# Window attention on one core: a new order of the stages in a slot, and smaller loads

## The chip, the cores and the metric

The kernel runs on one core of one Trainium2 chip. The metric is the device time of that core in microseconds (us). Before the change it is 4291.93 us, the median of 3 runs (4291.89 to 4298.81). All times below are of runs in the fast state, except one single run, whose state is unknown and which is marked. Most results are given as a ratio with a 95% interval, against runs of the kernel before on the same chip in the same rounds.

## The reference

```
x : (1, 511, 511, 192) bf16       window 7 x 7, 4 heads of 48
xp = pad(x, 1 on each side)
x0 = x + sum over i, j of xp[i : i+H, j : j+W] * dw_pe[i, j]      # depthwise 3x3
h  = layernorm(x0)                                                  # over the 192 channels
q, k, v = windows_of(h) @ w_qkv                                     # 73 x 73 windows of 49 tokens
out = softmax(q k^T / sqrt(48)) v,  @ w_o,  back to the image
return x0 + out
```

## The kernel before

Up to 128 windows lie on the 128 partitions and make a **block**. There are 42 blocks: 41 full or nearly full ones, and a ragged one of 81 windows. A block is worked off in 16 **slots** of 8 windows (11 in the last), 667 slots in all. While slot by slot the attention of block b runs, the same slots carry the convolution and then the LayerNorm (LN) of block b+1, and SyncE issues the loads of block b+2. The stages of a slot have letters in the code: A0 and A1 make q and k, V the values, B the scores and their exponential, D the product of the probabilities with v (one slot late), E the transposition of its result o (two slots late).

```python
for g in range(NG + LE + 1):                  # one turn is one slot
    # ... f0, f: how far the slot is within its block, from 0 to 1
    pj = []
    if 1 <= b and ck >= LE:
        goal = 13 if b == NB else part(0.10, 0.68, 13)      # 13 projections of block b-1
        # ...
    def hook(share):        # statistics for VectorE, stores and loads for SyncE
        # ...
        if n and conv.c == C:
            n.stats(int(s_start + (s_goal - s_start) * share))
        # ...
            goal = part(0.45, 0.82, len(xp), at)              # patches, 18 loads
            # ...
                goal = part(0.80, 0.90, len(xl), at)          # x, 4 loads
    if g < NG:
        stage_A(b, ck, 0, fill)               # q; fill() puts convolution matmuls between
        hook(0.15)
    if 0 <= g - LE < NG:
        stage_E(*groups[g - LE], nc.vector.tensor_copy)
    if g < NG:
        stage_A(b, ck, 1, fill)               # k
        hook(0.35)
    for s0 in pj:
        proj(b - 1, s0, ...)
    hook(0.55)
    now[0] = g + 0.5
    if n and g < NG:
        n.transpose(part(0.57, 0.95, WS), 0.9)    # LN transpose T of one row of block b+1
    if 0 <= g - LD < NG:
        stage_D()
    if g < NG:
        stage_B()
        hook(0.75)
        stage_V(b, ck, fill, nc.scalar.copy)
        # ...
```

The loads. Each window lies on one partition of X. The image rows of the windows are loaded in two pieces per line of windows:

```python
def load_x(self, b):
    for r0, r1 in ((0, 4), (4, WS)):          # 4 rows of 7, then 3
        for p, at in self.strips(b, r0, r1):  # two lines of windows per block
            # ... one nc.sync.dma_start each: 672 KB or 504 KB
```

The LN of a row of windows takes statistics on VectorE, then three steps on GpSimd (`tensor_scalar`, `pow`, and the multiplication that gives h), then the transpose T on TensorE, whose result is copied into HO half by VectorE and half by ScalarE. The tensors of a slot share a ring of three double banks of PSUM (`PS`). T and the convolution have their own two banks.

## Time and profile before

| | before |
|---|---|
| time, median | 4291.93 us |
| TensorE busy, mean granted clock | 85%, 0.91 |
| time at half clock in the profiled run | 771 us of 4282.5 |
| blocks 1 to 34, mean | 97.1 us |
| blocks 35 to 38 (tall ones are loaded and worked on) | 109.5, 120.0, 115.8, 115.4 us |
| block 39 (the ragged one is loaded), block 40, the last to the end | 138.5, 99.0, 79.8 us |

Times of blocks and slots here and below come from the starts of the 667 exponentials in the trace: "interval 8" is the mean, over blocks 1 to 33, of the time from the exponential of slot 8 to that of slot 9; interval 15 leads into the next block. "Half clock" sums the stretches for which the trace records a granted clock below full speed.

Two more lines of the wait table of the kernel before matter later (engine, line and tile, what it waited for: us in total, times, longest):

```profile
PE ps L369 <- DVE o L438: 91.0, 207, 0.8
...
PE ps L407 <- ACT k L377: 29.4, 78, 0.7
```

They are small waits of 0.4 us each, five and two in a block: q waits for VectorE, which frees a PSUM bank with o, and the scores wait for the eviction of k. And these are the x loads on the page's list of DMA issues (tile and source, engine, times, KB each):

```profile
X<-in_x_dram SPq DMA_DIRECT2D x82, 672.0 KB
X<-in_x_dram SPq DMA_DIRECT2D x82, 504.0 KB
```

### The profile page before, as it was taken

The numbers are of one execution on the slowest core, as the hardware profiler recorded it, in microseconds if no ns is written. First come the engines' busy times: TensorE is split into PE (matmuls) and PEld (weight loads), VectorE is DVE, ScalarE is ACT, GpSimd is POOL, SyncE is SP. The second block draws the span as 40 slices with busy tenths as digits, with TensorE's granted clock in tenths as the row PEclk, the third lists the DMA queues.
The fourth block names the chain that finished last, engine by engine and source line by source line (L and its number), as shares of the span: only waits on it lengthen the run. The fifth ranks groups of instructions, "written<-read, shape, count | busy, mean of one in ns | idle before, by whom it ended". The sixth has DMA issues, their size and how long they took to land.

```text
span 4282.5 us, 166362 instructions
## 1 busy us (share of the span) xinstructions
PE 3637.9 (85%) x75049; PEld 3180.5 (74%) x75049; DVE 2548.2 (60%) x4238; ACT 2779.9 (65%) x3508; POOL 2061.2 (48%) x1428
## 2 busy tenths in 40 slices
PE   4888888888989898888888888888889987777867
PEld 3777777777777787777777777777777876666656
DVE  6665666665565666666566566666656655555534
ACT  1666676666666677767666666766766665555646
POOL 4244455554444455555444445555544444444434
PEclk9998999999898899999999899999988997888878
DMA  5233344444333334444333333444433333333211
GB/s 121 62 85 85 91 97 97 105 102 99 84 85 85 85 91 95 103 107 104 91 85 85 85 91 91 98 98 104 106 86 85 85 84 84 84 84 71 54 43 43
DMA packets 522734, 376.91 MB, mean 88 GB/s; under 512 B 447216, under 2 KB 447408, under 8 KB 522014
## 3 DMA queue, kind: packets, MB, share of 16 engines
q1 hardware_dynamic: 521548, 365.89, 37.3%
q8 instruction: 589, 9.65, 0.9%
q14 instruction: 131, 1.07, 0.1%
q10 hardware_dynamic: 466, 0.30, 0.0%
HBM read 265.31 MB, written 100.27 MB: 85 GB/s over the span
## 4 chain that ended last, share of the span: by engine, by line
PE 51%; POOL 15%; DVE 10%; ACT 9%; SPq 6%; issue 5%; DMA 3%; ACTq 0%; POOLq 0%; DVEq 0%
PE ps L369 17%; PE psc L314 10%; PE ps L385 8%; POOL h L337 6%; ACT pO L475 6%; PE ps L452 6%; SPq L236 5%; POOL X L479 4%; PE ps L464 4%; POOL rstd L335 4%; DVE o L438 3%; PE psc L347 3%; DMA X<-in_x_dram 3%; DVE bnst L325 2%; ACT k L377 2%
## 5 line engine op out<-in xcount | busy, mean ns | idle before, releaser
L479 POOL TENSOR_TENSOR X<-X,pO 128x768 bf16<-128x768 bf16 (+1 forms) x539 | 836.6, 1565 | 1855.5 <-ACT pO L475 1853.9
L369 PE MATMUL ps<-HO,Wqk 96*128 96x392 bf16 x5336 | 1454.5, 357 | 100.1 <-DVE o L438 91.0
L314 PEld LDWEIGHTS <-XP 81*128 81x128 bf16 x8064 | 1117.6, 176 | 254.0 <-issue 191.9
L314 PE MATMUL psc<-T,XP 81*128 81x49 bf16 x8064 | 1100.6, 220 | 141.4 <-DMA XP<-in_x_dram 53.9
L377 ACT CAST k<-ps 128x784 bf16<-128x784 f32 x667 | 541.8, 812 | 477.9 <-PE ps L369 456.1
L369 PEld LDWEIGHTS <-Wqk 96*128 96x128 bf16 x5336 | 605.3, 117 | 261.5 <-issue 159.6
L385 PE MATMUL ps<-Wv,HO 96*128 96x192 bf16 x5336 | 687.5, 259 | 122.9 <-ACT pO L475 95.4
L377 ACT CAST q<-ps 128x784 bf16<-128x784 f32 x667 | 544.0, 816 | 316.2 <-PE ps L369 266.5
L453 DVE COPY HO<-ps 96x784 bf16<-96x784 bf16 x667 | 381.9, 573 | 614.9 <-PE ps L452 551.2
L320 DVE TENSOR_TENSOR X<-psc,X 128x490 bf16<-128x490 f32 x840 | 541.4, 645 | 321.6 <-PE psc L314 257.6
L337 POOL TENSOR_TENSOR h<-X,rstd 128x1344 bf16<-128x1344 bf16 x291 | 707.7, 2432 | 22.8
L393 ACT CAST v<-ps 128x768 bf16<-128x768 f32 x667 | 536.7, 805 | 234.8 <-PE ps L385 211.8
L438 DVE TENSOR_TENSOR o<-ps,rs 128x768 bf16<-128x768 f32 x667 | 638.7, 958 | 23.5
L415 ACT ACTIVATE pt<-ps 128x784 bf16<-128x784 f32 x667 | 550.9, 826 | 124.1 <-PE ps L407 121.0
L385 PEld LDWEIGHTS <-HO 96*128 96x128 bf16 x5336 | 520.7, 107 | 122.5 <-issue 94.0
L357 DVE COPY HO<-psc 96x896 bf16<-96x896 bf16 x294 | 339.0, 1153 | 323.8 <-PE psc L347 322.1
L325 DVE BATCH_NORM_STATS2 bnst<-X 128x6 f32<-128x384 bf16 x1050 | 518.1, 547 | 3.0
L452 PEld LDWEIGHTS <-o 128*96 128x96 bf16 x5336 | 422.1, 137 | 53.8 <-issue 8.6
L452 PE MATMUL ps<-ident,o 128*96 128x128 bf16 x5336 | 456.2, 234 | 3.9 <-issue 2.5
L464 PE MATMUL ps<-Wo,HO 96*128 96x192 bf16 x4116 | 454.2, 260 | 0.8 <-DVE HO L453 0.7
L357 ACT COPY HO<-psc 96x896 bf16<-96x896 bf16 x294 | 324.1, 1102 | 194.1 <-PE psc L347 152.1
L335 POOL TENSOR_TENSOR rstd<-tmp,expo 128x7 f32<-128x7 f32 x294 | 436.7, 1485 | 24.5
(54 smaller groups left out, 2872.0 us busy)
## 6 DMA issues: line engine op xcount, KB each, us to landing
XP<-in_x_dram SPq DMA_DIRECT2D x568, 216.0 KB
out_dram<-X SPq DMA_DIRECT2D x246, 336.0 KB
X<-in_x_dram SPq DMA_DIRECT2D x82, 672.0 KB
X<-in_x_dram SPq DMA_DIRECT2D x82, 504.0 KB
XP<-in_x_dram SPq DMA_DIRECT2D x151, 212.6 KB
out_dram<-X SPq DMA_DIRECT2D x82, 168.0 KB
XP<-in_x_dram SPq DMA_DIRECT2D x16, 192.0 KB
XP<-in_x_dram SPq DMA_DIRECT2D x64, 30.4 KB
```

What stands on the lines that cost most here:

```text
L314: mm(cv.ps[:, (c % 10) * S : (c % 10 + 1) * S], lhsT=XP[0:KP, :, c], rhs=T[0:KP, c, :], start=True, stop=True)
L325: nc.vector.bn_stats(out=bnst[:, s : s + 2, :].rearrange("p a f -> p (a f)"), in_=self.X[b % 3][:, s : s + 2, :].rearrange("p s c -> p c s"),)
L335: e.tensor_tensor(out=rstd[:, t], in0=tmp1[:, t], in1=expo[:, t], op=ALU.pow)
L337: eng.tensor_tensor(out=h[:], in0=self.X[b % 3][:, t, :], in1=rstd[:, t].unsqueeze(2).to_broadcast([128, WS, C]), op=ALU.mult)
L357: eng(out=HO[b % 2][0:KT, kt, :, r * WS : (r + 1) * WS], in_=pb[kt][:, 0 : WS * 128].rearrange("p (s w) -> p w s", w=128),)
L369: mm(ps[:, ab * 512 : ab * 512 + TOK], lhsT=self.Wqk[kt][0:KT, which * 2 + ab, :], rhs=HO[b % 2][0:KT, kt, ck * CH : (ck + 1) * CH, 0:S], ...
L377: nc.scalar.copy(out=dst[:, :, 0:TOK], in_=two_bank(ps, TOK))
L385: mm(ps[:, col : col + C], lhsT=HO[b % 2][0:KT, kt, w : w + 2, :].rearrange("p w s -> p (w s)"), rhs=self.Wv[kt][0:KT, :], start=(kt == 0) ...
L438: nc.vector.tensor_tensor(out=o_[:].rearrange("p b q (h d) -> p b (q h) d", d=DH), in0=ov[:, :, :, 0:DH], in1=r_[:].rearrange("p (b g) -> ...
L452: mm(ev, lhsT=o_[:, sl, Q, kt * KT : (kt + 1) * KT], rhs=ident[:], start=True, stop=True, is_transpose=True)
L464: mm(ps[:, col : col + C], lhsT=HO[b % 2][0:KT, kt, :, s0 + i], rhs=self.Wo[kt][0:KT, :], start=(kt == 0), stop=(kt == 1))
L479: nc.gpsimd.tensor_tensor(out=xv, in0=xv, in1=o[:, 0:n, :], op=ALU.add)
```

## The change

The intent is to take TensorE's waits away: T goes to the end of the slot, so that GpSimd has longer for h; V moves up behind k, with two v buffers; the projection ends earlier in the block, so that GpSimd's additions are over before LN begins; x comes in single rows; the tall lines begin at the second row, so that their loads need no cut at the image's top; the patch buffer is no longer cleared at the start, and the first loads go out before the setup.

```diff
 def _blocks(nwr, nwc):
+    top = min(1, nwr - tall)
-    halves += [(0, b, 1, 0, tall) for b in range(full, nwc)]
+    halves += [(top, b, 1, 0, tall) for b in range(full, nwc)]
-        for a in range(tall, nwr):
+        for a in [*range(top), *range(top + tall, nwr)]:
@@ start @@
-        nc.vector.memset(self.XP[:, 0:88, :], 0.0)
-        nc.gpsimd.memset(self.XP[:, 88:BLK, :], 0.0)
+        for t in list(self.load_xp(0)) + list(self.load_x(0)):     # before the setup, not after it
+            t()
@@ load_x @@
-        for r0, r1 in ((0, 4), (4, WS)):
+        for r0, r1 in [(r, r + 1) for r in range(WS)] if len(_blocks(self.NWR, self.NWC)[b]) <= 2 else [(0, WS)]:
@@ buffers; LN of block 0 @@
-        v_ = pool.tile([128, 4, NH, S], BF, name="v")
+        vv = [pool.tile([128, 4, NH, S], BF, name=f"v{i}") for i in range(2)]
-            h = hr.next()
+            h = self.X[2][:, t, :] if b == 0 else hr.next()
-                while n_.si < goal and len(n_.ready) - n_.tr < 2:
+                while n_.si < goal and len(n_.ready) - n_.tr < (2 if n_.b else WS):
@@ slot @@
-                goal = 13 if b == NB else part(0.10, 0.68, 13)
+                goal = 13 if b == NB else part(0.10, 0.56, 13)
-                    goal = part(0.45, 0.82, len(xp), at)
+                    goal = part(0.45, 0.78, len(xp), at)
-                        goal = part(0.80, 0.90, len(xl), at)
+                        goal = part(0.74, 0.95, len(xl), at)
                 stage_A(b, ck, 1, fill)
                 hook(0.35)
+                stage_V(b, ck, fill, nc.scalar.copy, vv[g % 2])
+                while n and conv.c < conv_goal:
+                    conv_mm(conv)
+                hook(0.55)
             for s0 in pj:
                 proj(...)
-            hook(0.55)
-            now[0] = g + 0.5
-            if n and g < NG:
-                n.transpose(part(0.57, 0.95, WS), 0.9)
             if 0 <= g - LD < NG:
-                stage_D()
+                stage_D(vv[(g - LD) % 2])
             if g < NG:
                 stage_B()
+                now[0] = g + 0.5
                 hook(0.75)
-                stage_V(b, ck, fill, nc.scalar.copy)
                 if n:
-                    while conv.c < conv_goal:
-                        conv_mm(conv)
+                    n.transpose(part(0.57, 0.95, WS), 1.0)
                     hook(1.0)
# cut: room for the second v buffer (smaller tmp1, expo; the zero tile moved into T),
# and the clears of the image's edge, which block 0 now needs too
```

The lines of the kernel after are one higher in most places: L370 is q and k (before L369), L386 V (L385), L408 the scores (L407), L429 D (L428), L348 T (L347).

More of the change, by code (lines that the diff above doesn't have):

```diff
@@ L75, in __init__ @@
         self.XPr = self.XP[0:KP].rearrange("(r q) n c -> q r n c", q=9)
-        nc.vector.memset(self.XP[:, 0:88, :], 0.0)
-        nc.gpsimd.memset(self.XP[:, 88:BLK, :], 0.0)
+        counts = [max(ln[4] + ln[5] for ln in blk) for blk in _blocks(self.NWR, self.NWC)]
+        if counts[0] < BLK:
+            nc.vector.memset(self.XP[:], 0.0)
         self.ident = consts.tile([128, 128], BF, name="ident")
-        self.zero = consts.tile([16, C], BF, name="zero")
-        nc.vector.memset(self.zero[:], 0.0)
         self.T = big.tile([128, C, S], BF, name="T")
+        nc.vector.memset(self.T[96:112, 0:4, :], 0.0)
+        self.zero = self.T[96:112, 0:4, :].rearrange("p c s -> p (c s)")
         self.X = [big.tile([128, S, C], BF, name=f"X{i}") for i in range(3)]
@@ L86, in __init__ @@
         gi = consts.tile([1, 1], I32, name="gi")
+        for i, t in enumerate(self.X):
+            if len(counts) <= i or counts[i] < BLK:
+                nc.gpsimd.memset(t[:], 0.0)
+        for t in list(self.load_xp(0)) + list(self.load_x(0)):
+            t()
         with tc.tile_pool(name="setup", bufs=1) as setup:
@@ L175, in __init__ @@
             nc.vector.tensor_copy(out=gi[:], in_=gm[:])
-        counts = [max(ln[4] + ln[5] for ln in blk) for blk in _blocks(self.NWR, self.NWC)]
-        for i, t in enumerate(self.X):
-            if len(counts) <= i or counts[i] < BLK:
-                nc.gpsimd.memset(t[:], 0.0)
-        for t in list(self.load_xp(0)) + list(self.load_x(0)):
-            t()
         cond = nc.values_load(gi[0:1, 0:1], min_val=0, max_val=1)
@@ L208, in load_xp @@
             right = [] if b0 + (n - 1) * db < NWC - 1 else list(range(n)) if da else [n - 1]
-            if left and any(ln[1] for bb in blocks[:b] for ln in bb):
+            if left and (b == 0 or any(ln[1] for bb in blocks[:b] for ln in bb)):
                 yield clear(XPr[0], p0, n if da else 1)
-            if right and b:
+            if right:
                 yield clear(XPr[8], p0 + right[0], len(right))
@@ L218, in load_xp @@
                 top, bot = a0 + i * da == 0, a0 + (j - 1) * da == NWR - 1
-                if top and b:
+                if top:
                     yield clear(XP[0:9], p0 + i, j - i)
-                if bot and b:
+                if bot:
                     yield clear(XP[KP - 9 : KP], p0 + i, j - i)
@@ L260, in fast @@
         rstd = pool.tile([128, S], F32, name="rstd")
-        tmp1 = pool.tile([128, S], F32, name="tmp1")
-        expo = pool.tile([128, S], F32, name="expo")
+        expo = pool.tile([128, 1], F32, name="expo")
         nc.vector.memset(expo[:], -0.5)
@@ L273, in fast @@
         nc.vector.memset(k_[:], 0.0)
-        for t in (pt, v_):
+        for t in [pt] + vv:
             nc.vector.memset(t[:], 1.0)
@@ L333, in ln_norm @@
             e = nc.gpsimd
-            e.tensor_scalar(out=tmp1[:, t], in0=bnst[:, t, 2], scalar1=1.0 / C, scalar2=self.eps, op0=ALU.mult, op1=ALU.add)
-            e.tensor_tensor(out=rstd[:, t], in0=tmp1[:, t], in1=expo[:, t], op=ALU.pow)
-            h = hr.next()
+            e.tensor_scalar(out=rstd[:, t], in0=bnst[:, t, 2], scalar1=1.0 / C, scalar2=self.eps, op0=ALU.mult, op1=ALU.add)
+            e.tensor_tensor(out=rstd[:, t], in0=rstd[:, t], in1=expo[:].to_broadcast([128, WS]), op=ALU.pow)
+            h = self.X[2][:, t, :] if b == 0 else hr.next()
             eng.tensor_tensor(
-                out=h[:], in0=self.X[b % 3][:, t, :], in1=rstd[:, t].unsqueeze(2).to_broadcast([128, WS, C]), op=ALU.mult
+                out=h[:, :, :], in0=self.X[b % 3][:, t, :], in1=rstd[:, t].unsqueeze(2).to_broadcast([128, WS, C]), op=ALU.mult
             )
@@ L377, in stage_A, with stage_V @@
             nc.scalar.copy(out=dst[:, :, 0:TOK], in_=two_bank(ps, TOK))
-        def stage_V(b, ck, fill, eng):
+        def stage_V(b, ck, fill, eng, v_):
             ps = PS.next()
@@ L417, in stage_B, with stage_D @@
             )
-        def stage_D():
+        def stage_D(v_):
             ps = PS.next()
```

## The prediction

> **What bounds the kernel now.** I read the page first, then the wait table, then the order of time inside one block, then the tables by stretch. The page gives the frame:
>
> ```profile
> PE 3637.9 (85%) x75049; PEld 3180.5 (74%) x75049; DVE 2548.2 (60%) x4238; ACT 2779.9 (65%) x3508; POOL 2061.2 (48%) x1428
> PEclk9998999999898899999999899999988997888878
> PE 51%; POOL 15%; DVE 10%; ACT 9%; SPq 6%; issue 5%; DMA 3%; ACTq 0%; POOLq 0%; DVEq 0%
> q8 instruction: 589, 9.65, 0.9%
> ```
>
> TensorE is busiest, but its clock is never granted in full for a whole slice, and GpSimd holds 15% of the chain that ended last though it works 48% of the span. So the tensor work is interrupted. The program is 42 blocks of windows (41 of 16 slots, one of 11: 667 slots, one exponential each). Block b computes attention on block b, convolution (first 45%) and LN (second half) of block b+1, and loads block b+2. The starts of the 667 exponentials date the slots: first at 107.4 us, block 1 at 202.7, block 35 at 3504.4, last block at 4203. Blocks 1 to 34 take (3504.4 - 202.7) / 34 = 97.1 us each; blocks 35 to 39 take 109.5, 120.0, 115.8, 115.4 and 138.5. Who stops TensorE:
>
> ```profile
> PEld L347 <- POOL h L337: 146.2, 85, 7.2
> PE ps L385 <- ACT pO L475: 95.4, 321, 1.1
> PE ps L407 <- issue: 49.8, 15, 4.5
> PE psc L314 <- DMA XP<-in_x_dram: 53.9, 5, 13.5
> PE psc L314 <- DMA X<-in_x_dram: 48.7, 3, 37.7
> DVE X L320 <- DMA X<-in_x_dram: 53.3, 9, 8.4
> ```
>
> (engine and line, what it waited for: us in total, times, longest.) These are four different things: LN transposes that wait for GpSimd's h; V that waits for an eviction of the projection; waits for nothing visible; and loads. In order of time, from blocks 20 and 39 (start, length, instruction, in brackets the idle time before it):
>
> ```profile
> 2103.64 1.26 PE L347 MATMUL psc<-ident,h 128*96 128x128 bf16 x14 [2.36 <-POOL h L337]
> 2113.54 3.18 SPq L250 DMA_DIRECT2D X<-in_x_dram  x4
> 2126.09 1.28 PE L385 MATMUL ps<-Wv,HO 96*128 96x192 bf16 x7 [4.14 <-issue]
> 4097.87 0.35 PE L314 MATMUL psc<-T,XP 81*128 81x49 bf16 x2 [37.72 <-DMA X<-in_x_dram]
> ```
>
> The first stop is there in slot 10 of every block I looked at, 2.35 us each time. The second falls in slots 13 to 15 of 28 of the first 33 blocks, 1.6 to 4.5 us, always while the four x loads of 504 and 672 KB, issued within 3.2 us, move. The third is in the blocks that load the column ("tall") blocks and the rest. The stops cost more than their length:
>
> ```profile
> 2101.00:2111.00 10.00, 7.64 (x109) 5.78 (x108) 5.00 (x9) 4.62 (x7) 9.17 (x9) 0.66 0.70 192
> 2122.00:2132.00 10.00, 5.91 (x45) 4.44 (x48) 2.09 (x5) 3.54 (x5) 2.60 (x2) 0.66 0.64 133
> 2132.50:2144.00 11.50, 10.05 (x239) 9.19 (x228) 7.01 (x13) 6.89 (x10) 0.00 (x0) 1.00 0.01 4
> ```
>
> (stretch, length, busy time and instructions of PE, PEld, DVE, ACT, POOL, then clock.) After each stop the mean clock of ten us is 0.66, without one it is 1.00. Block 20's slots are 6.0 6.4 5.9 6.6 6.0 6.7 4.8 4.5 6.9 5.5 7.2 6.6 4.7 4.9 10.7 5.7 us: a slot with LN and no stop takes 4.7; the GpSimd stop makes two of them 7.2 and 6.6 (4.4 us lost), the other makes one 10.7 (6 us lost, 4.14 of it idle).
>
> **What the Trainium skill says.** (1) "TensorE: Matmul & The Clock Gate", section "What's actually happening": the clock falls to half after an idle window and returns after a busy one, windows about 3.4 us. The trace agrees with the half clock after stops, but here 2.35 us of idleness suffices. (2) "Runtime: NRT & Kernel Launch", section "Instruction fetch mechanics": instructions stream in by DMA in 16 KiB blocks of 256. The trace agrees: 589 packets, 9.65 MB, 16,384 bytes each, on queue 8; in block 20 one came at 2101.86, the next at 2111.98 and 2123.30, against about 6 us apart elsewhere, and the wait of 4.14 us ended after the last. So I read "issue" here as TensorE out of instructions, its fetch standing behind x on the same 16 engines. (3) "DMA: Bandwidth & Descriptors", section "Queues, rings and completion order": engines go round robin between queue rows by packet. That should protect the fetch; the trace shows that it does not fully.
>
> **The change part by part.** TensorE's order in a slot was q, E, k, projection, LN transpose, D, scores, V; it becomes q, E, k, V, projection, D, scores, LN transpose, with two v buffers.
>
> LN transposes last: V (0.82), D (0.26) and scores (0.36 us, all by start to start in block 20) now run before the transpose, 1.4 us of cover for the 2.36. Projection by 56% instead of 68% of a block: its 13 steps fall in slots 2 to 8, not 2 to 10, so GpSimd's adds (1.65 us each, L479) no longer stand between LN's 0.21 + 1.49 + 2.43 = 4.13 us per row. GpSimd then needs 4.13 us in slots of 4.7, and slot 10's stop goes: 4.4 us per block.
>
> x row by row: 14 loads of 168 KB from 74% to 95% instead of 4 from 80% to 90%. The block's 2.35 MB took some 11 us at about 215 GB/s in a burst; spread over 14 us or more it leaves the fetch room. SyncE pays 14 x 0.65 = 9 us instead of 3.2, beside 18 patch loads at 1.27 (23 us) and stores: it fits into the 38 us that half a block gives, barely. I count 4.5 us per block gained on average, and 1 us of remainder paid.
>
> V after k: 1.1 us more between k's end and the scores, which waited 29.4 us in all for the k eviction (78 times); and V stands before, not after, the projection's evictions (95.4 us). Against that, E now starts only 1.8 us after D in a convolution slot where o takes 1.94 us, and two projections end on ScalarE's evictions. By slots: two convolution slots without projection 4.9; five with two projections 6.7 (before 6.6); slot 7 4.9; slot 8 5.3; seven LN slots 4.75, which DVE, ACT and PE all nearly fill. Sum 9.8 + 33.5 + 4.9 + 5.3 + 33.3 = 86.8, plus 1 remainder: 88 us per block.
>
> Tall lines from the second row: no cut at the top, so 18 patch loads per block instead of 36 and no clears; blocks 35 to 38 become 88. The last block's load stays 81 pieces and 11 clears at 0.81 us: from 39 us of block 39 that is 39 + 75 + 4, so TensorE resumes near 121 and block 39 takes 127. Its x is 9 pieces, not 18: block 40 takes 92 instead of 99.
>
> No cleared patch buffer, first loads early: patch loads start near 1 us, not 9.75, but x (first before, 0.8 us) now comes after them and the clears wait for landings, so the first add stays near 45 us (before 44.7). LN of block 0 writes into a free X and is not paced by two buffers: 61.6 to 101.9 becomes some 26 us, but the convolution of block 1 waits for its x, about 97. Gain 8 us.
>
> Sum: blocks 1 to 34, 34 x 9.1 = 309; blocks 35 to 39, 599 - (4 x 88 + 127) = 120; block 40 7; start 8; the rest 2. 446 from 4292 is 3846; I say 3845.
>
> **The rivals.** (a) The fetch still starves: with 14 more issues SyncE is nearly always busy and the rows bunch up at the end of the block, so the stop moves to slot 15 or to the next block's first convolution. For it: SyncE's sum above; against it: at most eight loads are in flight, 1.4 MB. It would cost back 3 to 4.5 us in 36 blocks: 3950 to 4010. (b) A new wait takes V's place: E on o, or the projection's two evictions on ScalarE, in seven slots of each block. For it: ScalarE's sum in such a slot is six instructions of 0.8 us, 4.9 us in a slot of 6.4; against it: convolution fills TensorE. Half a us in each of seven slots: 3.5 us per block, 3975. (c) The last block's load hides after all, or LN slots fall to DVE's own sum of 4.3 us: 3740 to 3800. (d) Nothing gained because VectorE or ScalarE bound all slots: the clean slots of 4.7 beside stopped ones of 7 speak against it.
>
> **Range and chances.** 3845 us; 3725 to 3990 holds (c) and most of (a) or (b) alone. Both together would still be some 4140, over 2% faster. Faster by over 2%: 0.95; within: 0.04; slower: 0.01.
>
> **What would show it.** Right: no idle over 1.5 us before L347 in slot 10; no "issue" stop over 1.5 us in slots 13 to 15; clock near 0.97; regular blocks of 86 to 90 us; tall ones alike, block 39 alone near 127; V no longer waiting for pO. Wrong: the clock still near 0.91, fetch packets 10 us apart, E (L452 before) waiting for o, convolution adds waiting for x at block starts, or block 39 without a stall.

## The result, and the profile after

The kernel after takes 3987.18 us, the median of 3 runs (3961.14 to 3999.06). The ratio is 0.927, interval 0.920 to 0.935. (Ratios here are the mean time of one kernel's fast runs over that of the other's of the same rounds, so not quite the ratio of the medians quoted.) It is within the stated range, at its upper end, and 142 us above the predicted 3845.

The page of the kernel after, to be set beside the first lines of the prediction: busy time of the engines, clock in 40 slices, the chain that ended last, the instruction fetch queue, and the x loads.

```profile
PE 3495.5 (88%) x75049; PEld 3059.4 (77%) x75049; DVE 2529.0 (63%) x4238; ACT 2798.6 (70%) x3508; POOL 2052.4 (51%) x1427
...
PEclk9989899999999999999999999999989998999888
...
q8 instruction: 589, 9.65, 1.0%
...
PE 52%; DVE 25%; ACT 11%; DMA 4%; SPq 3%; issue 3%; POOL 1%; ACTq 0%; DVEq 0%; POOLq 0%
...
X<-in_x_dram SPq DMA_DIRECT2D x574, 168.0 KB
```

The same 75,049 matmuls take 142 us less busy time, since fewer of them run at half clock (mean clock 0.953; 380 us at half clock instead of 771). GpSimd, named with 15% of the chain before, now has 1%, with the same work. VectorE has taken its place: 25% instead of 10%.

The waits of the kernel after:

```profile
PE ps L429 <- DVE HO L454: 130.8, 201, 1.0
...
PE ps L370 <- ACT pO L476: 69.1, 238, 1.4
...
DVE X L321 <- DMA X<-in_x_dram: 54.5, 12, 12.6
PEld L453 <- DVE o L439: 51.5, 130, 1.6
...
PE psc L315 <- DVE X L321: 47.1, 14, 11.6
PE ps L370 <- DVE HO L358: 44.4, 38, 1.2
PE psc L315 <- DMA XP<-in_x_dram: 39.9, 1, 39.9
...
PE ps L408 <- issue: 4.1, 5, 1.5
```

T (L348) no longer waits for h in the table, and the scores' wait for nothing visible has gone from 49.8 to 4.1 us. In blocks 0 to 32 no "issue" stop of TensorE over 1.5 us is left; there were 28, 84.6 us in sum (one of them, 2.4 us in block 23, the trace puts down to an x load instead). V (L386) does not wait for pO any more. Instead four waits are new: D for E's eviction (L454), in five slots of a block; q for pO; E for o (L453); and q for an eviction of T (L358), once per block.

This last one, at the end of block 21, in order of time (start, length, instruction, idle before it):

```profile
2086.66 0.98 PE L348 MATMUL psc<-ident,h 128*96 128x128 bf16 x14
...
2087.70 1.08 DVE L358 COPY HO<-psc 96x896 bf16<-96x896 bf16 x1
2088.84 0.34 PE L370 MATMUL ps<-HO,Wqk 96*128 96x392 bf16 x1 [1.20 <-DVE HO L358]
```

T of the last LN row stands last in the last slot. Its copy ends at 2088.78, and the very next thing on TensorE is q of the next block, which needs all seven rows of HO: TensorE stands still for 1.20 us.

Two stretches of that block, with LN and the patch loads, then with LN and the x loads (stretch, length, busy us and instructions of PE, PEld, DVE, ACT, POOL, then clock, DMA share, GB/s), and SyncE's issues there:

```profile
2060.00:2070.00 10.00, 8.78 (x207) 6.87 (x206) 8.72 (x16) 8.58 (x12) 9.57 (x7) 1.00 0.66 165
2072.00:2082.00 10.00, 8.59 (x240) 6.80 (x227) 8.70 (x15) 8.26 (x10) 8.31 (x7) 1.00 0.84 188
```

```profile
2058.40 13.59 SPq L238 DMA_DIRECT2D XP<-in_x_dram  x11
...
2074.94 11.66 SPq L252 DMA_DIRECT2D X<-in_x_dram  x13
```

The clock is 1.00 through both stretches. Nearly all x rows of a block go out within 12 us, 0.9 us each, while the engines are 0.84 busy: this is not the gentle spreading that the prediction had in mind, yet nothing starves.

Block 39, where the 81 patch loads and 11 clears of the ragged block are issued, and the wait for its x behind it:

```profile
3793.81 0.36 PE L315 MATMUL psc<-T,XP 81*128 81x49 bf16 x2 [39.86 <-DMA XP<-in_x_dram]
...
3809.67 1.24 DVE L321 TENSOR_TENSOR X<-psc,X 128x490 bf16<-128x490 f32 x2 [12.63 <-DMA X<-in_x_dram]
```

By slots, the regular block adds up as follows (us; interval 1 ends with the exponential of slot 2, so intervals 1 to 5 answer to the prediction's slots 2 to 6, intervals 8 to 14 to its seven LN slots 9 to 15):

| intervals | before | predicted | after |
|---|---|---|---|
| 1 to 5: convolution, two projections | 32.1 | 33.5 | 33.7 |
| 6 | 4.9 | 4.9 | 4.8 |
| 7 | 4.5 | 5.3 | 5.3 |
| 8 to 14: LN slots | 42.4 | 33.3 | 33.1 |
| 15 and 0: end of a block, beginning of the next | 13.3 | 9.8 (+ 1 remainder) | 13.6 |
| sum | 97.1 | 88 | 90.5 |

The gain is in the LN slots, and in sum it is as predicted there; the miss of the regular block is in the row of the boundary. But the rows do not hold the same work before and after: T of a slot now runs after the slot's exponential, so interval 8 has no T any more and interval 15 has one. What that does to the comparison is said below, at "Sum ... 88 us per block".

### The profile page after: what moved, and what is told of

Its sections match the earlier page's. It is cut to its first block, busy times and chain, and to the rows that moved or that the text cites. A ratio compares the mean times of both kernels' runs of the same rounds, so it can differ in the third digit from the quotient of the medians.

```text
span 3985.4 us, 165790 instructions
## 1 busy us (share of the span) xinstructions
PE 3495.5 (88%) x75049; PEld 3059.4 (77%) x75049; DVE 2529.0 (63%) x4238; ACT 2798.6 (70%) x3508; POOL 2052.4 (51%) x1427
## 3 DMA queue, kind: packets, MB, share of 16 engines
q8 instruction: 589, 9.65, 1.0%
## 4 chain that ended last, share of the span: by engine, by line
PE 52%; DVE 25%; ACT 11%; DMA 4%; SPq 3%; issue 3%; POOL 1%; ACTq 0%; DVEq 0%; POOLq 0%
PE ps L370 16%; PE psc L315 11%; ACT pO L476 8%; PE ps L386 8%; DVE bnst L326 8%; DVE o L439 6%; PE ps L453 6%; PE ps L465 6%; DVE HO L358 6%; DMA X<-in_x_dram 4%; PE ps L429 4%; DVE HO L454 3%; DVE rs L438 2%; SPq L238 2%; ACT v L394 2%
## 5 line engine op out<-in xcount | busy, mean ns | idle before, releaser
L370 PE MATMUL ps<-HO,Wqk 96*128 96x392 bf16 x5336 | 1397.7, 345 | 130.2 <-ACT pO L476 69.1
L315 PE MATMUL psc<-T,XP 81*128 81x49 bf16 x8064 | 1076.1, 220 | 111.9 <-DVE X L321 47.1
L370 PEld LDWEIGHTS <-Wqk 96*128 96x128 bf16 x5336 | 566.7, 112 | 202.3 <-DVE HO L358 54.6
L386 PE MATMUL ps<-Wv,HO 96*128 96x192 bf16 x5336 | 651.1, 249 | 28.1 <-ACT q L378 22.1
L386 PEld LDWEIGHTS <-HO 96*128 96x128 bf16 x5336 | 526.3, 106 | 154.9 <-issue 117.9
L438 DVE RECIPROCAL rs<-ps 128x16 f32<-128x16 f32 x667 | 171.7, 257 | 706.6 <-PE ps L429 624.3
L454 DVE COPY HO<-ps 96x784 bf16<-96x784 bf16 x667 | 379.5, 569 | 336.0 <-PE ps L453 335.9
L326 DVE BATCH_NORM_STATS2 bnst<-X 128x6 f32<-128x384 bf16 x1050 | 520.1, 547 | 3.0
L453 PEld LDWEIGHTS <-o 128*96 128x96 bf16 x5336 | 388.3, 131 | 83.1 <-DVE o L439 51.5
L336 POOL TENSOR_TENSOR rstd<-rstd,expo 128x7 f32<-128x7 f32 x294 | 434.9, 1479 | 24.5
L453 PE MATMUL ps<-ident,o 128*96 128x128 bf16 x5336 | 436.5, 227 | 9.3 <-DVE o L439 4.9
L465 PE MATMUL ps<-Wo,HO 96*128 96x192 bf16 x4116 | 442.9, 261 | 0.7 <-DVE HO L454 0.7
L476 ACT CAST pO<-ps 128x768 bf16<-128x768 f32 x498 | 387.0, 800 | 51.6 <-PE ps L465 33.0
```

What stands on the lines that cost most here:

```text
L315: mm(cv.ps[:, (c % 10) * S : (c % 10 + 1) * S], lhsT=XP[0:KP, :, c], rhs=T[0:KP, c, :], start=True, stop=True)
L326: nc.vector.bn_stats(out=bnst[:, s : s + 2, :].rearrange("p a f -> p (a f)"), in_=self.X[b % 3][:, s : s + 2, :].rearrange("p s c -> p c s"),)
L370: mm(ps[:, ab * 512 : ab * 512 + TOK], lhsT=self.Wqk[kt][0:KT, which * 2 + ab, :], rhs=HO[b % 2][0:KT, kt, ck * CH : (ck + 1) * CH, 0:S], ...
L386: mm(ps[:, col : col + C], lhsT=HO[b % 2][0:KT, kt, w : w + 2, :].rearrange("p w s -> p (w s)"), rhs=self.Wv[kt][0:KT, :], start=(kt == 0) ...
L453: mm(ev, lhsT=o_[:, sl, Q, kt * KT : (kt + 1) * KT], rhs=ident[:], start=True, stop=True, is_transpose=True)
L465: mm(ps[:, col : col + C], lhsT=HO[b % 2][0:KT, kt, :, s0 + i], rhs=self.Wo[kt][0:KT, :], start=(kt == 0), stop=(kt == 1))
```

## The experiments

Twelve kernels were run, in four batches; all gave correct results. Those that start from the kernel before have names with b, those from the kernel after with a. Except where noted, each was timed in 3 rounds; the kernel before gave medians of 4266.64, 4271.82, 4276.04 and 4274.04 us beside the four batches. At the record's threshold of 2%, the early projection alone and the spread pieces count as "same" and the order alone and the tall lines alone as "unclear", though their intervals lie below 1; the other timed runs are "faster".

### One part alone: projection early

```diff
-                goal = 13 if b == NB else part(0.10, 0.68, 13)
+                goal = 13 if b == NB else part(0.10, 0.56, 13)
```

> The kernel before with one constant changed: the projection's steps spread over 10 to 56% of a block instead of 10 to 68%. Theory: slot 10's stop (2.35 us of idle and the half clock after it, 4.4 us a block) exists because the projection's adds stand in GpSimd's queue between the rows of LN; with the adds gone by slot 8 the stop is gone: 41 x 4.4 = 180 us less, about 4110 us, no idle of over 1.5 us before L347 in steady blocks. Rival: the stop is there because the transpose comes too early in the slot, whatever GpSimd does beside it: the 2.35 us stay and the time is 4265 to 4300.

Measured: 4224.01 us, ratio 0.987 (0.980 to 0.994), between the two expectations. Its waits of T for h:

```profile
PEld L347 <- POOL h L337: 132.9, 85, 7.2
```

Before it was 146.2 us in as many waits. So the wait did not vanish when GpSimd's additions left its way: TensorE waits 1.47 us in one block looked at, one slot earlier, instead of 2.36. The stops over 1.2 us are still 44, with 79.5 us in sum instead of 115.0. The regular block takes 94.7 us instead of 97.1. The prediction's reason for this part (GpSimd then needs 4.13 us in slots of 4.7, so the stop goes) is too simple.

### One part alone: the order in the slot

V after k with two v buffers, T after the scores; all else as before.

```diff
+                stage_V(b, ck, fill, nc.scalar.copy, vv[g % 2])
+                ...                                    # rest of the convolution, hook(0.55)
-            hook(0.55)
-            now[0] = g + 0.5
-            if n and g < NG:
-                n.transpose(part(0.57, 0.95, WS), 0.9)
-                stage_D()
+                stage_D(vv[(g - LD) % 2])
-                stage_V(b, ck, fill, nc.scalar.copy)
+                    n.transpose(part(0.57, 0.95, WS), 1.0)
```

> The kernel before with the order of a slot alone changed: V after k with two v buffers, LN transposes last (and the small buffers that make room). Theory: slot 10's stop shrinks below 1 us because 1.4 us of other work now stands ahead of the transpose, V's wait for the projection's eviction (95 us in all) goes, and in exchange each block's last transpose is followed at once by the next block's q, a wait of about 1.2 us for its eviction in 41 blocks: a net gain of 100 to 170 us, 4120 to 4190 us. Rival: only the projection's place removes slot 10's stop, and the boundary wait eats the rest: 4260 to 4320 us.

Measured: 4214.14 us, ratio 0.985 (0.978 to 0.992), again between the two expectations. Lines of its wait table (here T is L346, q L368):

```profile
PEld L346 <- POOL h L336: 59.4, 45, 7.2
...
PEld L368 <- DVE HO L356: 42.6, 38, 1.3
```

The wait for h has fallen by more than half, and from block 1 on none is over 0.95 us: the order alone takes slot 10's stop away. In its place q's wait for the eviction of T at the block's end appears at once, with nothing else changed: it belongs to the order. The regular block takes 95.4 us.

### One part alone: x row by row

```diff
-        for r0, r1 in ((0, 4), (4, WS)):
+        for r0, r1 in [(r, r + 1) for r in range(WS)] if len(_blocks(self.NWR, self.NWC)[b]) <= 2 else [(0, WS)]:
-                        goal = part(0.80, 0.90, len(xl), at)
+                        goal = part(0.74, 0.95, len(xl), at)
```

> The kernel before with x loaded in 14 pieces of one row from 74 to 95% of a block instead of 4 pieces from 80 to 90%. Theory: the waits named issue in slots 13 to 15 are TensorE's instruction fetch standing behind the burst of x; spread out they go: about 4.5 us a block in 34 blocks, some 150 us less, 4140 us, no issue stop over 1.5 us in slots 13 to 15. Rival: what counts is the sum of bytes in the second half, so the stops stay or move to the next block's first convolution, 4270 to 4320 us.

Measured: 4103.6 us, ratio 0.959 (0.953 to 0.966). This is the largest part, 163 us against the 4266.64 of its batch. The regular block takes 92.4 us, 4.7 less than before, and one "issue" stop over 1.5 us is left of 28. T's wait for h is unchanged (146.6 us), so the two cures act on different stops.

### One part alone: tall lines from the second row

```diff
+    top = min(1, nwr - tall)
-    halves += [(0, b, 1, 0, tall) for b in range(full, nwc)]
+    halves += [(top, b, 1, 0, tall) for b in range(full, nwc)]
-        for a in range(tall, nwr):
+        for a in [*range(top), *range(top + tall, nwr)]:
```

> The kernel before with the tall lines on rows 2 to 65. Theory: 18 patch loads instead of 36 and no clears in the blocks that load tall lines: their block time falls from 110 to 120 to about 105 (the trace after the whole change shows them some 8 us above regular ones), and the last block's load stays: 50 to 80 us less, 4215 to 4245 us. Rival: it is not the number of loads but how slowly each tall load moves, then under 25 us less, 4265 us or more.

Measured: 4224.12 us, ratio 0.986 (0.979 to 0.994). The regular block stays at 97.4 us; blocks 35 to 38 fall from 115 to 103 us on average (105.2, 105.3, 98.3, 101.4). The four parts alone gain 43 + 52 + 163 + 42 = 300 us, and the whole change 305, so nothing over some 25 us, by which the medians of the kernel before differ between batches, is missing from them, though they overlap where both the order and the projection treat the wait for h.

### Small pieces, or spread out?

Two runs take the x part apart. One keeps the rows, but issues them in the old, short window (80% to 90% of the block); the other keeps the four big pieces and spreads them over the new window.

```diff
 # rows in a burst: only the loop over single rows, the window stays
                         goal = part(0.80, 0.90, len(xl), at)
 # four pieces spread: only the window
-                        goal = part(0.80, 0.90, len(xl), at)
+                        goal = part(0.74, 0.95, len(xl), at)
```

> The kernel before with x in 14 pieces of one row, but still from 80 to 90% of a block. Theory: it is the spreading that spares the instruction fetch, so in a burst the stops of slots 13 to 15 come back, at least in part: 4180 to 4260 us. Rival: smaller pieces alone do it, because each is issued separately and at most eight are in flight: 4095 to 4125 us, as with the spread rows.

> The kernel before, x still in 4 pieces of 504 and 672 KB, but spread from 74 to 95% of a block. Theory: what starves the instruction fetch is the bytes queued ahead of it; a burst of 4 pieces queues some 8 us of work (2.35 MB issued in 3.2 us, moved at about 215 GB/s), while rows are issued at 0.76 us each, no faster than they move. Four pieces spread out queue at most about 3 us each, so most stops of slots 13 to 15 go: 4105 to 4160 us. Rival: the piece's own size counts (one piece of 672 KB suffices for a stop), then the stops stay and the time is 4210 to 4290.

Measured: rows in a burst 4099.02 us, ratio 0.960 (0.956 to 0.964), as good as the spread rows of the run before. Four pieces spread 4220.07 us, ratio 0.988 (0.983 to 0.993). The burst, as SyncE issues it and in a table of ten us:

```profile
2014.21 10.65 SPq L250 DMA_DIRECT2D X<-in_x_dram  x14
```

```profile
2015.00:2025.00 10.00, 8.73 (x213) 7.13 (x212) 8.24 (x14) 8.42 (x11) 7.93 (x6) 1.00 0.99 223
```

The DMA engines are 0.99 busy for ten us, at 223 GB/s, and TensorE does its work at full clock. That is as full as the same stretch with the four pieces in the kernel before, block 20, which is followed by the 4.14 us stop:

```profile
2114.00:2124.00 10.00, 7.41 (x197) 5.94 (x195) 8.57 (x15) 7.73 (x10) 7.57 (x6) 1.00 1.01 197
```

With the spread pieces SyncE takes 7.15 us for three of them, and the scores still wait for nothing visible.

```profile
PE ps L407 <- issue: 27.3, 10, 4.3
```

Of the 28 stops over 1.5 us, 15 are left with the spread pieces and none with the burst of rows. So smaller pieces are enough, with the engines as busy as before; spreading the big pieces takes only about half of the stops away.

What differs is how much is waiting at once. From the traces, in blocks 1 to 33 (means; "waiting" is the largest sum of bytes that SyncE had issued and the DMA engines had not yet moved while x was loaded; stops are those over 1.5 us in blocks 0 to 32):

| | x from issue to landing | waiting | stops |
|---|---|---|---|
| kernel before: four pieces | 11.8 us | 2.4 MB | 28 |
| four pieces spread | 10.3 us | 1.8 MB | 15 |
| rows in a burst | 5.2 us | 0.8 MB | 0 |
| rows spread | 5.8 us | 0.9 MB | 1 |
| kernel after: rows spread | 4.9 us | 0.7 MB | 0 |
| kernel after with four pieces (next run) | 11.6 us | 2.4 MB | 22 |

SyncE takes eight semaphores in turn for its transfers, so at most eight are in flight, whatever their size; that limits the rows, and not the four pieces. The spread pieces did not do what their expectation assumed (some 3 us of queued work each): they stood nearly as deep as the burst. The packets of x have 2688 bytes in all of these runs, so the size of the packets is not the reason.

That the stops are TensorE's instruction fetch can be read from the packets of the instruction queues, here of the kernel before:

```profile
q8 instruction: 589, 9.65, 0.9%
q14 instruction: 131, 1.07, 0.1%
```

Queue 8 is TensorE's stream: 9.65 MB for its 2 x 75,049 instructions is 64 bytes each, and the 16,264 instructions of all other engines fit queue 14 in the same way (66 bytes each). Each of the 27 "issue" stops ends 1.2 to 1.7 us after a packet of queue 8 has landed. By chance about 8 in 100 would, since that is the share of time within such a distance of a packet's end. The packets themselves take at most 1.9 us; but 63 of the intervals between their starts in blocks 0 to 32 are over 9 us before, and 28 with the burst. The delay lies before a packet starts. That it grows with what is waiting fits all six runs; by what way, the traces do not show.

### The changed kernel with the four pieces put back

```diff
-        for r0, r1 in [(r, r + 1) for r in range(WS)] if len(_blocks(self.NWR, self.NWC)[b]) <= 2 else [(0, WS)]:
+        for r0, r1 in ((0, 4), (4, WS)):
-                        goal = part(0.74, 0.95, len(xl), at)
+                        goal = part(0.80, 0.90, len(xl), at)
```

> The changed kernel with x again in 4 pieces from 80 to 90% of a block. Theory: the stops for instructions come back in slots 13 to 15 of most blocks, 80 to 180 us more: 4070 to 4160 us. Rival: with the patch loads ended earlier (78 instead of 82%) and SyncE busier the pieces no longer stand in one burst, 3970 to 4030 us.

Measured: 4132.1 us, ratio 0.965 (0.961 to 0.970), against 0.927 for the kernel after: 145 us are lost (4132.1 - 3987.2, of different batches). 22 stops over 1.5 us come back in blocks 0 to 32, 78.0 us in sum, and in the wait table the scores' wait for nothing visible:

```profile
PE ps L408 <- issue: 50.6, 16, 4.9
```

### The changed kernel with the projection late again

```diff
-                goal = 13 if b == NB else part(0.10, 0.56, 13)
+                goal = 13 if b == NB else part(0.10, 0.68, 13)
```

> The changed kernel with the projection back at 10 to 68% of a block. Theory: the parts add up as they did from the kernel before, so the late projection costs some 40 us, 4020 to 4040, with slots 8 and 9 longer. Rival: once the transposes go last the projection's place no longer matters, 3975 to 4000 us, or it even helps because slots 2 to 6 hold fewer pairs of projections.

Measured: 3971.12 us, the median of three fast runs (3958.92 to 3994.36; a fourth, 4028.11, counts as slow and is left out), ratio 0.931 (0.924 to 0.938). It cannot be told from the kernel after. With the new order T waits for h 39 times, at most 0.9 us, where it did 2.36 us before. So once the order is changed, the early projection is worth nothing: intervals 1 to 5 are 1.7 us shorter with the late one, and interval 8 is as much longer. The last block is 4 us shorter (80.2 us instead of 84.3).

### The changed kernel with the last T early

The wait of q at the block's end can be taken away by moving the T of the last slot in front of D, where D and the scores follow it.

```diff
+            if n and f == 1.0 and g < NG:
+                now[0] = g + 0.5
+                n.transpose(WS, 1.0)
             if 0 <= g - LD < NG:
                 stage_D(vv[(g - LD) % 2])
```

> The changed kernel, but the last transpose of each block stands before D in slot 15, not after the scores. Theory: the 1.2 us idle at each block's end, where the next block's q waits for the eviction of that transpose, goes, and with it the half clock that follows it in some 20 blocks: slot 15 falls from 8.1 us to about 6 and slots 0 and 1 lose their slow ones, 90.5 to about 87 us a block, 3850 to 3890 us in all. Rival: the convolution at the block's start waits for the last x rows anyway, so the stop only changes its name: 3950 to 3990 us.

Measured: 3932.82 us, ratio 0.922 (0.918 to 0.926); some 54 us below the kernel after, against 3850 to 3890 expected. The two are of different batches, and the intervals of their ratios overlap (0.927, 0.920 to 0.935, for the kernel after); in the traces the regular block takes 89.1 us instead of 90.5, which over 33 blocks is 47 us. The wait is gone:

```profile
PEld L370 <- DVE HO L358: 10.1, 39, 0.3
```

Intervals 14, 15 and 0 sum to 17.0 us instead of 18.1. Of the 33 boundaries from block 1 to block 33, 12 are still followed by half clock within 9 us of the exponential of slot 15 (17 in the kernel after, 191 us in sum; now 102 us). In 8 of the 12 another wait of 1.0 to 3.1 us stands before it, which the kernel after has too; in the other 4 TensorE has no stop over 0.25 us there, and the cause is open. The convolution of the new block needs x rows that were issued last:

```profile
DVE X L321 <- DMA X<-in_x_dram: 75.7, 23, 11.1
...
PE psc L315 <- DVE X L321: 67.1, 24, 10.1
```

The first is VectorE's addition waiting for the rows, the second the convolution on TensorE waiting for that addition. In the kernel after they were 54.5 us in 12 waits and 47.1 us in 14. TensorE comes to the boundary earlier, and the rows do not. So part of the gain turned into waiting for them, as the rival had it, and the size expected was too large.

### The start: statistics of block 0 paced as before

```diff
-                while n_.si < goal and len(n_.ready) - n_.tr < (2 if n_.b else WS):
+                while n_.si < goal and len(n_.ready) - n_.tr < 2:
```

> The changed kernel with block 0's LN paced again, at most two normalised rows ahead of the transposes (they still go to the free X). Theory: in the changed kernel all seven rows of statistics stand in VectorE's queue ahead of the first eviction of a transpose, so TensorE idles 21.9 us; paced, the first exponential comes at about 103 to 106 us instead of 111.9. Rival: GpSimd's chain of about 4.8 us a row sets the pace either way, and the first exponential stays within 2 us of 111.9.

Measured, one run only, state unknown: 3989.82 us. The first exponential comes at 108.4 us instead of 111.9, between the two expectations. The reason for the late start in the kernel after is this instruction:

```profile
93.67 1.65 PE L348 MATMUL psc<-ident,X 128*96 128x128 bf16 x14 [23.67 <-DVE HO L358]
```

The statistics of all seven rows stand in VectorE's queue ahead of the copy of the first T; TensorE waits 23.67 us for that copy. A gain of 3.5 us in a total that scatters by 38 us can only be read from the trace, not from the time.

### Three corrections together

The two last ones, and loads 8% of a block earlier, so that the rows land before the boundary.

```diff
+            if n and f == 1.0 and g < NG:
+                now[0] = g + 0.5
+                n.transpose(WS, 1.0)
-                while n_.si < goal and len(n_.ready) - n_.tr < (2 if n_.b else WS):
+                while n_.si < goal and len(n_.ready) - n_.tr < 2:
-                    goal = part(0.45, 0.78, len(xp), at)
+                    goal = part(0.45, 0.70, len(xp), at)
-                        goal = part(0.74, 0.95, len(xl), at)
+                        goal = part(0.66, 0.88, len(xl), at)
```

> The changed kernel with the block's last transpose before D, block 0 paced, and the loads earlier: patches from 45 to 70%, x from 66 to 88% of a block. Theory: what is left at block starts after the first repair is the last x rows that land late (the convolution's add waits for them); issued earlier they are there: 3870 to 3915 us, against 3933 with the first repair alone, and slots 15 and 0 near 5.2 and 4.9 us. Rival: SyncE issues the loads as fast as it can already and the earlier goals change nothing: 3920 to 3945 us.

Measured: 3896.2 us (3887.01 to 3912.01), ratio 0.910 (0.906 to 0.914). It is the best kernel of the study, 91 us below the kernel after (by the ratios of their batches, which do not overlap, some 74 us). Half clock follows 6 of the 33 boundaries. The regular block takes 88.4 us, and intervals 15 and 0 together 10.7 instead of 13.6. The wait of D for E's eviction is as long as ever:

```profile
PE ps L429 <- DVE HO L454: 131.7, 205, 1.0
```

### Statistics behind E's eviction

The wait just shown: E's eviction stands in VectorE's queue behind the LN statistics of the slot (L326, 0.5 us apiece). Is the order of the queue at fault, or is VectorE full?

```diff
                 stage_A(b, ck, 0, fill)
-                hook(0.15)
             if 0 <= g - LE < NG:
                 stage_E(*groups[g - LE], nc.vector.tensor_copy)
+            if g < NG:
+                hook(0.15)
@@ in hook @@
-                if n and conv.c == C:
+                if n and conv.c == C and (share < 1.0 or f == 1.0):
```

> Edit: the version with the last LN transpose early and the loads earlier (a_best, 3896 us), and in it the first batch of LN statistics of each slot is issued after E instead of before it, and the batch at the slot's end is left out (except in a block's last slot), so that statistics no longer stand in VectorE's queue ahead of E's eviction. My theory: D waits for that eviction (131.7 us in 205 waits there, slots 9 to 13) because of the order of VectorE's queue, not because VectorE is full. Then the waits of D on L454 fall below 60 us, the LN slots lose some 0.3 us each, 1.5 to 2 us per block, and the time is 3820 to 3865 us. Rival: VectorE is full in the LN slots (8.6 to 8.8 us busy of 10), so what E's eviction gains is paid by o, and by the statistics, which come later and make the LN transposes wait: D's waits fall but E's on o rise by about as much, and the time is 3880 to 3915 us. Second rival: the statistics come too late for the transposes, the last row's transpose in slot 15 waits for h, and the time is above 3915 us.

Measured: 4091.14 us, ratio 0.957 (0.952 to 0.962). It is a miss: 195 us slower than the version it started from, as only the second rival had it. D's wait for E's eviction is gone from the table altogether, and intervals 9 to 13, with as many T in them, shrink from 25.0 to 23.0 us. So the wait came from the order of the queue. But of the 18 statistics in these intervals two have moved on into interval 14, and VectorE's busy time there falls from 21.95 to 21.11 us: 0.8 us of the 2.0 is work that went elsewhere, and at most 1.1 us was idle time that the order cost. VectorE was 88% busy there and is 92% busy now, so the first rival is right in part. And the statistics come later. Those of the last row end 1.1 us before the exponential of slot 15, on average over blocks 1 to 33, where they ended 6.9 us before it; h comes later with them, and the last T, which waits for it, is back at the boundary. Interval 15 takes 12.6 us instead of 5.5. The end of block 20 in order of time:

```profile
2035.62 0.21 POOL L335 TENSOR_SCALAR rstd<-bnst 128x7 f32<-128x7 f32 x1 [3.82 <-DVE bnst L326]
2035.92 1.48 POOL L336 TENSOR_TENSOR rstd<-rstd,expo 128x7 f32<-128x7 f32 x1
2037.47 2.43 POOL L338 TENSOR_TENSOR h<-X,rstd 128x1344 bf16<-128x1344 bf16 x1
...
2039.96 1.73 PE L348 MATMUL psc<-ident,h 128*96 128x128 bf16 x14 [3.59 <-POOL h L338]
```

GpSimd sat idle for 3.82 us until the last row's statistics ended, then needed its 4.1 us, and TensorE waited 3.59 us of that. T itself then took 1.73 us, in place of 0.98, since the clock had fallen; half clock follows all 33 boundaries, 433 us in sum. A version that puts E's eviction first and begins the statistics earlier was not tried.

## Why the prediction was right or wrong, point by point

The direction and the causes named for the two largest stops held. The sum missed by 142 us. By the terms of the prediction's own sum, in the profiled runs:

| term | predicted | measured | difference |
|---|---|---|---|
| start and block 0, until block 1 begins | 194.7 us (202.7 - 8) | 192.8 us | -2 |
| blocks 1 to 34 | 34 x 88 | 34 x 90.7 | +91 |
| blocks 35 to 38 | 4 x 88 | 97.3 + 100.1 + 96.5 + 98.5 = 392.4 | +40 |
| block 39 | 127 | 144.1 | +17 |
| block 40 | 92 | 88.3 | -4 |
| last block and "the rest" | 77.8 (79.8 - 2) | 84.3 | +7 |

The differences add up to 149 us, as the spans of the profiled runs do (3985.4 against 4282.5 - 446 = 3836.5).

**"LN transposes last ... slot 10's stop goes: 4.4 us per block."** The stop went, in full. But the prediction gave the order and the early projection as joint reasons, and the runs separate them: alone, the projection leaves all 40 stops of the regular blocks in place, only shorter, and the order takes them away; in the changed kernel the projection's place is worth nothing.

**"x row by row ... spread over 14 us or more it leaves the fetch room."** The size is right: 4.5 us less 1 us were predicted, and the part alone gives 4.7 per block. The mechanism is wrong. A burst of rows is as good as spread rows, and spread pieces keep half the stops. The step should have been about how much stands queued at once: 2.4 MB with four pieces, 0.8 or 0.9 MB with rows, since at most eight loads are in flight. The prediction has this limit, but only as an argument against rival (a). (Its 2.35 MB are 2352 KB of 1024 bytes, 2.41 MB; nothing hangs on it.)

**"Sum ... 88 us per block."** The groups of slots within the block are right to 0.2 us. For the LN slots this is partly luck: the sum gave each of seven 4.75 us with a T, but interval 8 has none and takes 3.5, the other six average 4.93, and the seventh T lies in interval 15. Counted with it, LN is some 0.8 us over (33.1 + 1.0 - 33.3), and the boundary some 1.8 us. The term that failed is the "1 remainder" for the boundary. T in the last slot costs its own 1.0 us on top of the slot's 4.9, and after it q waits 1.2 us for the copy of T. So interval 15 is 7.1 us (4.9 + 1.0 + 1.2) in blocks without half clock, such as block 20, and 8.1 on average with it; interval 0 is 4.8 and 5.5. The prediction asked what T last would gain and not who needs T's result next. The runs with the last T early and the rows earlier give 88.4 us, near the 88 predicted.

**Rival (a): the stop moves "to slot 15 or to the next block's first convolution".** The place and the cost (3950 to 4010 us) came true, the cause did not: it is not the fetch, but the eviction of T, and then x rows that land late. The result lay in the range of this rival for another reason.

**Rival (b): a new wait takes V's place.** It came true in part. V's 95.4 us behind pO and q's 91.0 behind o are gone; D's 130.8 us behind E's eviction, q's 69.1 behind pO and E's 51.5 behind o have come. The prediction looked at ScalarE's load for this; the largest of the new waits is in VectorE's queue. It cost little in the sum: the last run shows that at most 1.1 us per block is in it.

**Rivals (c) and (d).** Neither came: block 39 stalls, and the LN slots with a T take 4.93 us, not 4.3.

**"Tall lines from the second row ... blocks 35 to 38 become 88."** The mechanism held, 18 patch loads per block instead of 36, and the blocks became 12 to 20 us shorter (4 to 18 with this part alone; regular ones became 6.6 shorter by the rest). The term was mis-sized: the prediction gave these patch loads the duration of the ordinary ones, and they are slower. In block 37 of the kernel after SyncE's issue and the DMA share are

```profile
3528.41 19.85 SPq L238 DMA_DIRECT2D XP<-in_x_dram  x11
```

```profile
3530.00:3546.00 16.00, 13.46 (x371) 10.67 (x370) 13.69 (x25) 13.39 (x17) 14.69 (x12) 1.00 0.51 110
```

1.80 us each instead of 1.24 (13.59 / 11), with the engines half busy. The x rows then follow so late that the next block's convolution waits for them. Why these loads move at 110 GB/s, where the ordinary ones beside LN move at 165, is open.

**Block 39, "39 + 75 + 4".** The stall came: TensorE stood still for 39.9 us on the ragged block's patches. The loads began 42.5 us into the block instead of 39, stores in between took 3.2 us, and TensorE resumed at 125 instead of 121; x, in pieces of nine partitions, came after them: another 12.6 us, which the sum did not have.

**Block 40, "Its x is 9 pieces, not 18".** The gain came (88.3 us against 92 predicted), but not for this reason: with the order alone the block takes 88.3 us, with the x rows alone, where x is in 9 pieces too, 99.4. The last block is 4.5 us longer, not 2 shorter; with the early projection alone it is 85.3 us.

**The start, "Gain 8 us".** The first exponential came 4.5 us later, not earlier, because of the statistics in VectorE's queue. Yet block 0 took 80.9 us instead of 95.3, so that block 1 began 9.9 us earlier; the size came out near the predicted one by an account that the prediction did not make. With the x rows alone block 0 already takes 83.8 us, so most of it belongs to them.

**What would show it.** Of its signs of being right, the two kinds of stop over 1.5 us are gone and V no longer waits for pO. The clock (0.953, not 0.97), the regular block (90.5, not 86 to 90), the tall blocks and block 39 (144) miss. Of its signs of being wrong, E waits for o (51.5 us), and the convolution's additions wait for x (54.5 us, where it was 53.3 before).

## What to carry to other kernels

When an instruction is moved to the end of a loop's turn to hide what it waits for, look up who consumes its result in the next turn: the cover gained in front is lost behind, and here it came back as 1.2 us and a lower clock per block until the last one alone was moved forward. When a large load seems to starve something else, try smaller pieces in the same window before spreading or moving it, because what is queued at once can matter more than how busy the engines are; where the number of loads in flight is limited, as to eight here, smaller loads also mean that fewer bytes wait. And in a queue that is worked off in order, as VectorE's was here, putting one thing first delays all others: check the longest chain that starts from those others before taking a short wait away.

## What the Trainium skill lacked or had wrong

- "TensorE: Matmul & The Clock Gate", section "HAM oscillation — how this bites in real kernels", gives the abstract rule that TensorE must not idle for more than about 3.4 us; no page gives a length for the short idle times between groups of matmuls of which it also speaks. Here stops of 2.36 us in the kernel before were followed by ten us at a mean clock of 0.66, and of the boundaries of the changed kernel, with idle times of 1.2 us, 17 of 33 were followed by half clock of 3.4 us or more (in 3 of the 17 after a second stop of 0.9 to 1.9 us). The clock also falls after shorter stops, and not after all of them.
- "Runtime: NRT & Kernel Launch", section "Instruction fetch mechanics", calls the cost of crossing a 16 KiB boundary mostly hidden. Here it was not, as long as x came in four loads of 504 and 672 KB: 27 stops of 1.6 to 4.5 us in 33 blocks, each ended 1.2 to 1.7 us after a packet of TensorE's instruction queue had landed, and none when the same bytes came in a burst of 14 loads.
- "DMA: Bandwidth & Descriptors", section "Rules for kernel authors", advises 1 MiB per DMA for bandwidth, and does not say what large loads do to other traffic. Here ten us with 168 KB loads, and patch loads beside them, reached 223 GB/s at 0.99 busy, where ten us with loads of 504 and 672 KB reached 197 GB/s at 1.01 in the kernel before, and the kernel with the burst was 173 us faster.
- No page that was read explains why the patch loads of the tall lines take 1.80 us each at a DMA share of 0.51, where those of the ordinary lines take 1.24 us at 0.66.
